# First layer's gate and value products, from the fourth pair of column blocks on, as seven block products in place of eight, on all engines in one planned order

## The chip, the cores and the metric

The kernel runs on one core of a Trainium2 chip. The metric is device microseconds of one execution; less is better. Several executions are timed, and one more is taken by the hardware profiler.

## The reference

Pooled attention (2 batches, 8 heads, 1152 tokens of 64, queries pooled in pairs) gives x of 1152 tokens x 512. A gated layer follows, the part that is changed, and then a second gated layer with eight experts:

```python
def _moe_ref(x, w_gate, w_val, w_out):      # 512 -> 1536 -> 512
    gate = 1.0 / (1.0 + np.exp(-(x @ w_gate)))
    val = x @ w_val
    return (gate * val @ w_out).astype(np.float32)
```

w_gate, w_val and w_out arrive as float64. The second layer (`_moe2_ref`) computes for each of 8 experts max(x @ w1, 0) @ w2, weighted by a routing matrix that is normalised eight times over rows and columns.

## The kernel before

All matrices are kept as two parts of a reduced float32 format, a high part (a ScalarE copy that rounds) and a low part (the rest, a subtraction). A product is three matmuls, high x high, high x low and low x high, issued by `three` (L964, matmuls on L965 to L967). x lies transposed in four tiles `x1[c]` of 128 rows (features) x 1152 columns (tokens), high and low.

There are five stretches of work. **Attention** is an order of instructions written out by a planner: each instruction is a `step` with an engine, a due time `when`, its length, what it waits for and which buffers it takes and frees; `arrange` (L219) simulates the engines and gives one order for all of them, with a table of corrections to the due times (`SHIFT`), and the program keeps it (`tc.manual_schedule`, L951). The planner also has a `port` time, within which VectorE and GpSimd operations on SBUF are not started together. The **first layer's gate and value stage** (L975 to L1018) is not planned: a loop over `fc`, 12 pairs of 128 x 2 weight columns, issues its instructions, and the compiler orders them on each engine. `gate_weights` (L985) loads and converts the weights of a pair, first one block of the gate, then one of the value. A pair is 2 (gate, value) x 4 (feature tiles c) x 3 (thirds of the tokens) x 3 = 72 matmuls of 384 columns into PSUM tiles `psb` of three banks. Then a sigmoid reads the gate's banks (L1012, ScalarE), VectorE multiplies the value's banks by it (L1013), ScalarE copies the high part of g (L1016) and GpSimd subtracts for the low part (L1017). The **output layer** (L1036 to L1067) makes four blocks of 128 output features, each 12 x 3 x 3 = 108 matmuls of 384 columns into `pso`, over g of fc 0 to 11 in that order; its weights come from the same conversion. The **second layer** is planned again (`step` on L1101): a period of 45.4 us for each of 16 halves of an expert.

`split_doubles` (L181) converts 512 float64 weight columns: a scaled copy of the upper word into PSUM (L198, ScalarE), on VectorE the sign (L199) and a shift (L200), the high part (L204, ScalarE), on VectorE what is left (L205), sign and exponent (L206) and the lower word scaled by them (L208), and GpSimd adds both into the low part (L211). Raw words have 3 buffers (`rawp`, L961), scratch tiles 2 of a kind (`conv`, L214), converted weights 2 ring slots (`ring_tile`, L969).

The second layer's first product (`first_product`, L1216) already has the form that the change brings to the first layer: x and the weights are seen as 2 x 2 blocks, and seven products of sums of blocks, A11, S1, S2, A12, S3, S4 and A22, replace eight products of blocks. A product is 2 halves of the tokens' half x 2 feature tiles x 3 = 12 matmuls of 288 columns. The products are accumulated in bank pairs X, Y and B; A11 is copied from X (or Y) to B by ScalarE (`go`), further results are copied out by ScalarE (`tap`) or added by VectorE (`add`).

## Time and profile before

| | us |
|---|---|
| median of the runs shown (1253.24, 1253.52, 1257.1) | 1253.52 |
| the profiled execution: time | 1254.48 |
| the profiled execution: span, first to last instruction | 1252.7 |
| first layer's gate and value stage in it | 287.2 to 436.9 |
| output layer, first three blocks | 436.9 to 493.0 |

Engines are PE (TensorE), PEld (its weight loads), DVE (VectorE), ACT (ScalarE), POOL (GpSimd) and SP (which issues DMAs). Busy time of PE is time with a matmul in flight; consecutive matmuls overlap, so the step from start to start, not the duration, is the cost of one. The granted clock (PEclk) is a share of 2.4 GHz. L numbers are lines of the kernel before; helper lines (L1127 for a ScalarE copy, L1130 for a two-operand operation) hold many different instructions, which are told apart by their tiles.

### The profile page before, as it was taken

To read this page: it belongs to the slowest core of one execution; us is meant where nothing else is said; L and a number is where in the kernel's file an instruction comes from. 1 tells how busy PE (TensorE), PEld (TensorE's weight loads), DVE (VectorE), ACT (ScalarE), POOL (GpSimd) and SP (SyncE) were. 2 spreads that over 40 slices of the span, in tenths; PEclk is the share of its full clock that TensorE was granted. 3 is DMA by queue.
4 is the path that set the end of the run, shared out by engine and by line. 5 is a ranking of instruction groups with operands and counts; after the bars stand their busy time and mean duration, and the time that the engine had idled before them with its cause. 6 is when DMAs were issued, how large, how long until landed. Compare 5 with 4: busy or idle time off the path is not lost.

```text
span 1252.7 us, 23722 instructions
## 1 busy us (share of the span) xinstructions
PE 1236.4 (99%) x8924; PEld 1204.6 (96%) x8924; DVE 1072.9 (86%) x1954; ACT 780.5 (62%) x1775; POOL 719.0 (57%) x751
## 2 busy tenths in 40 slices
PE   7999999999999999999999999999999999999998
PEld 7889999999999999999999999999999999999998
DVE  7999999998666674899998898898889889889887
ACT  8999999994333332657457457547556645745753
POOL 7788888674434432753574555464555556456552
PEclk9999999999999999999999999999999999999999
DMA  5112211112222232111111111111111111111112
GB/s 161 43 54 58 59 48 38 37 51 68 84 85 85 90 96 68 35 52 35 34 52 52 51 52 35 52 52 51 35 51 52 51 52 35 51 52 52 34 35 77
DMA packets 62357, 70.50 MB, mean 56 GB/s; under 512 B 3489, under 2 KB 49953, under 8 KB 62241
## 3 DMA queue, kind: packets, MB, share of 16 engines
q1 hardware_dynamic: 62240, 68.97, 18.0%
q8 instruction: 70, 1.15, 0.4%
q14 instruction: 47, 0.38, 0.1%
HBM read 66.60 MB, written 2.36 MB: 55 GB/s over the span
## 4 chain that ended last, share of the span: by engine, by line
PE 78%; DVE 14%; ACT 4%; POOL 1%; issue 1%; DMA 1%; SPq 0%; DVEq 0%; ACTq 0%; POOLq 0%
PE psb L965 4%; PE psb L967 4%; PE psb L966 4%; PE psY L965 4%; PE psY L966 4%; PE psY L967 4%; PE psX L965 4%; PE psX L966 3%; PE psX L967 3%; PE psX L1391 3%; PE psX L1396 3%; PE psX L1395 3%; DVE pT L517 3%; PE psY L1391 3%; PE psY L1396 3%; PE psY L1395 3%
## 5 line engine op out<-in xcount | busy, mean ns | idle before, releaser
L1130 POOL TENSOR_TENSOR sm<-xs 128x512 f32<-128x512 f32 x64 | 92.7, 1459 | 165.1 <-ACT xs L1127 150.2
L1127 ACT ACTIVATE w_two<-sm 128x512 fp32r<-128x512 f32 x128 | 77.8, 629 | 162.9 <-POOL sm L1130 141.2
L1130 POOL TENSOR_TENSOR sm<-raw_w 128x256 f32<-128x256 f32 x128 | 105.0, 842 | 125.1 <-DMA raw_w<-in_moe_w_dram 84.5
L536 PE MATMUL psg<-pT,vs 128*128 128x256 f32 (+1 forms) x576 | 133.4, 319 | 1.0 <-DVE pT L517 0.8
L1130 DVE TENSOR_TENSOR hb<-sm,hb 128x512 fp32r<-128x512 f32 x128 | 120.6, 969 | 9.2 <-ACT hb L1127 9.2
L1130 DVE TENSOR_TENSOR w_two<-sm,w_two 128x512 fp32r<-128x512 f32 x128 | 111.0, 874 | 5.7 <-ACT w_two L1127 5.6
L1127 ACT ACTIVATE hb<-sm 128x512 fp32r<-128x512 f32 x128 | 75.8, 626 | 55.2 <-POOL sm L1130 53.9
L1391 PE MATMUL psX<-w_two,hb 128*128 128x256 f32 x384 | 108.8, 283 | 0.2 <-DVE acc L1346 0.2
L1391 PE MATMUL psY<-w_two,hb 128*128 128x256 f32 x384 | 108.5, 283 | 0.0
L1395 PE MATMUL psX<-w_two,hb 128*128 128x256 f32 x384 | 108.3, 282 | 0.0
L1395 PE MATMUL psY<-w_two,hb 128*128 128x256 f32 x384 | 108.3, 282 | 0.0
L1396 PE MATMUL psX<-w_two,hb 128*128 128x256 f32 x384 | 108.0, 281 | 0.1
L1396 PE MATMUL psY<-w_two,hb 128*128 128x256 f32 x384 | 108.0, 281 | 0.0
L517 DVE TENSOR_TENSOR pT<-psg,pT 128x384 fp32r<-128x384 f32 x192 | 101.8, 550 | 6.7 <-ACT pT L513 4.9
L497 PE MATMUL psg<-ident,p 128*128 128x128 f32 x648 | 104.3, 273 | 1.0 <-DVE pT L517 0.8
L536 PEld LDWEIGHTS psg<-pT,vs 128*128 128x128 f32 x576 | 91.3, 189 | 4.6 <-POOL sum L549 0.9
L1130 POOL TENSOR_TENSOR sm<-raw_w,sm 128x256 f32<-128x256 f32 x96 | 95.5, 1007 | 0.3
L513 ACT ACTIVATE pT<-psg 128x384 fp32r<-128x384 f32 x192 | 90.9, 501 | 5.6 <-PE psg L497 4.3
L1130 DVE TENSOR_TENSOR w_two<-raw_w,w_two 128x512 fp32r<-128x512 f32 x96 | 73.6, 769 | 17.9 <-ACT w_two L1127 16.2
L965 PE MATMUL psb<-x,w_gv 128*128 128x384 f32 x264 | 88.2, 334 | 0.0
L966 PE MATMUL psb<-x,w_gv 128*128 128x384 f32 x264 | 88.2, 334 | 0.0
L967 PE MATMUL psb<-x,w_gv 128*128 128x384 f32 x264 | 88.2, 334 | 0.0
(282 smaller groups left out, 4731.6 us busy)
## 6 DMA issues: line engine op xcount, KB each, us to landing
raw_w<-in_moe_w_dram SPq DMA_DIRECT2D x64, 512.0 KB, 3.5
raw_o<-in_moe_w_out_dram SPq DMA_DIRECT2D x12, 512.0 KB, 3.5
raw_gv<-in_moe_w_gate_dram SPq DMA_DIRECT2D x11, 512.0 KB, 3.6
raw_gv<-in_moe_w_val_dram SPq DMA_DIRECT2D x11, 512.0 KB, 3.6
vr<-in_v_dram SPq DMA_DIRECT2D x16, 288.0 KB, 2.7
kr<-in_k_dram SPq DMA_DIRECT2D x15, 288.0 KB, 2.8
qr<-in_q_dram SPq DMA_DIRECT2D x15, 256.0 KB, 4.0
out_dram<-acc SPq DMA_DIRECT2D x18, 128.0 KB, 1.8
```

Source lines behind the costliest of these rows:

```text
L497: nc.tensor.transpose(have["tpp", i, u, g][:, n * P:(n + 1) * P], have["p", i, u][:, jj * P:(jj + 1) * P], ident)
L513: nc.scalar.activation(out=p_parts(i, u, g)[0], in_=turned(i, u, g), func=AF.Copy)
L517: nc.vector.tensor_tensor(out=lo, in0=turned(i, u, g), in1=f(hi), op=ALU.subtract)
L536: nc.tensor.matmul(have["pv", i, j, n][:, 0:HALF[n][1]], have["vs", i, j][:, jj].rearrange("p a d -> p (a d)"), have["pT", i, j, n][s][:, ...
L965: nc.tensor.matmul(ps, wh, xh, start=first, stop=False, skip_group_check=more)
L966: nc.tensor.matmul(ps, wh, xl, start=False, stop=False, skip_group_check=more)
L967: return nc.tensor.matmul(ps, wl, xh, start=False, stop=last, skip_group_check=more).ins
L1127: nc.scalar.activation(out=out_, in_=in_, func=func)
L1130: eng.tensor_tensor(out=out_, in0=a, in1=b, op=op)
L1391: nc.tensor.matmul(out_, h[:, 0, cols], w[:, 0], start=(begins and kk + m == 0), stop=False, skip_group_check=True,)
L1395: nc.tensor.matmul(out_, h[:, 0, cols], w[:, 1], start=False, stop=False, skip_group_check=True)
L1396: nc.tensor.matmul(out_, h[:, 1, cols], w[:, 0], start=False, stop=(m == 1), skip_group_check=True)
```

## The change

The first layer's gate and value stage gets a planner like the second layer's (the same `step`, now made by `planner`), with due times and a table of corrections, `SHIFT1` (571 entries, not shown). It is planned together with the conversion of the first output block's weights (`wo`). The first three units of work (NPL = 3) are computed as before, with 384 columns: gate and value 0, gate and value 1, gates 2 and 3. The nine others (values 2 and 3, gates 4 and 5, values 4 and 5, and so on) are blocks of seven products with 84 matmuls of 288 columns.

For these blocks GpSimd first adds high and low part of x again (`xq`), VectorE makes four differences of them (`tq`, each in two feature tiles), ScalarE their high parts (`th`) and GpSimd their low parts (`tl`). The conversion of a weight pair now makes whole float32 weights (`u`, GpSimd), GpSimd makes four sums of weight blocks from them, and the high and low parts of 1792 columns are made by ScalarE (`wh`) and VectorE (`wl`). VectorE adds S3 and S4 out of PSUM to earlier results (`add`). In a block of gates, sigmoids are taken by ScalarE out of PSUM or of these sums; in a block of values, VectorE multiplies A12's and A22's banks by the gate, and GpSimd multiplies the sums. The products g are kept as float32, and split later: g 0 to 3 within the plan by ScalarE and VectorE, g 4 to 11 behind it, where the high part of g takes the tile of the float32 g before it (`HOME`). Those eight splits (two low parts on GpSimd, six on VectorE) stand ahead of the output layer and are ordered by the compiler, as is all of the output layer. PSUM is eight single banks in the plan (X, Y, B and two for conversions), and the former pools are opened behind it.

```diff
+NPL = 3
...
-        def gate_weights(fc):
-            w = ring_tile(fc, f"gv{fc}")[:, :, 0:1024]
-            split_doubles(
-                w,
-                [src[:, fc * 2 * P:(fc + 1) * 2 * P].rearrange("(c p) f -> p c f", p=P) for src in (wg1, wv1)],
-                f"gv{fc}", ps_v,
-            )
-            parts[fc] = [w.rearrange("p s (i c f) -> p s i c f", i=2, c=KD)[:, :, i] for i in range(2)]
-        ring_tile(0, "gv0")
-        gate_weights(1)
-        for fc in range(NFF):
-            if fc > 1:
-                gate_weights(fc)
-            wr = parts[fc]
-            pss = []
-            for i in range(2):
-                ps = ps_b.tile([P, 3, 512], F32, tag="b", name="psb")
-                for c in range(KD):
...
+        xq = [area[f"l{8 + c}"] for c in range(KD)]
+        tx = [area[f"t{k}"] for k in range(4)]
+        gf = {fc: area[f"l{fc}"] for fc in range(8)}
+        gs = {}
...
+        HOME = ("h0", "h1"), ("h2", "l0"), ("l1", "wf"), ("l2", "sm"), *((f"l{fc - 1}", f"t{fc // 2 - 2}") for fc in range(4, NFF))
+        def home(fc, k):
+            tag = HOME[fc][k]
+            if tag[0] == "h":
+                return area[tag]
+            if tag[0] == "t":
+                if fc % 2 == 0:
+                    area["w" + tag] = g_p.tile([P, 2, N], F32R, tag=tag, name="gh")
+                return area["w" + tag][:, fc % 2]
+            return g_p.tile([P, N], F32R, tag=tag, name="gh")
+        def split_hi(fc):
+            hi = home(fc, 0)
+            gs[fc] = (hi,)
+            copy(hi, g32(fc))
+        def split_lo(fc, eng):
+            lo = home(fc, 1)
+            join(eng, lo, g32(fc), f(gs[fc][0]), ALU.subtract)
+            gs[fc] += (lo,)
+        stock1 = {
+            "raw": [rawp.tile([P, 512, 2], I32, tag="raw", name="raw_gv") for _ in range(3)],
+            "cv": [conv.tile([P, 512], F32, tag=t, name="cv") for t in ("da", "da", "ds", "ds", "dv", "dv")],
+            "w": rings,
+            "wf": [area["wf"]],
+            "sm": [area["sm"]],
+            "m": [misc.tile([P, N], F32, tag="m", name="sg") for _ in range(4)],
+        }
+            gate, val = (lambda fc: (wg1, fc)), (lambda fc: (wv1, fc))
+            units = [(gate(0), val(0)), (gate(1), val(1)), (gate(2), gate(3)), (val(2), val(3))]
+            for fc in range(4, NFF, 2):
+                units += [(gate(fc), gate(fc + 1)), (val(fc), val(fc + 1))]
+            def begins(fc):
+                return 12.5 * fc if fc < NPL else 12.5 * NPL + 10.95 * (fc - NPL)
+            def double(name, src, t, out):
...
+                    ("v", *name), "ACT", t, 530, 640,
+                    lambda: nc.scalar.activation(out=have[v], in_=f(have[raw][:, :, 1]), func=AF.Copy, scale=2.0 ** -112),
+                    [("ld", *name)], [("v", v)], [raw, v],
+                )
+                step(
+                    ("s", *name), "DVE", t + 0.7, 605, 690, lambda: nc.vector.tensor_scalar(
+                        out=have[a].bitcast(I32), in0=have[v].bitcast(I32), scalar1=SIGN, scalar2=None, op0=ALU.bitwise_and
+                    ), [("v", *name)], [("cv", a)], [v, a],
+                )
+                step(
+                    ("x", *name), "DVE", t + 1.3, 605, 690, lambda: nc.vector.scalar_tensor_tensor(
+                        out=have[a].bitcast(I32), in0=have[v].bitcast(I32), scalar=3, in1=have[a].bitcast(I32),
+                        op0=ALU.logical_shift_left, op1=ALU.bitwise_or,
+                    ), [("s", *name)], (), [v, a],
+                )
+                step(
+                    ("e", *name), "DVE", t + 1.9, 605, 690, lambda: nc.vector.tensor_scalar(
+                        out=have[v].bitcast(I32), in0=have[a].bitcast(I32), scalar1=SIGNEXP, scalar2=None, op0=ALU.bitwise_and
+                    ), [("x", *name)], (), [v, a],
+                )
+                step(
+                    ("t", *name), "DVE", t + 2.5, 605, 690, lambda: nc.vector.scalar_tensor_tensor(
+                        out=have[b], in0=have[raw][:, :, 0].bitcast(U32), scalar=2.0 ** -52, in1=have[v],
+                        op0=ALU.mult, op1=ALU.mult,
+                    ), [("e", *name)], [("cv", b)], [raw, v, b],
+                )
+                out_, gets, uses = out
+                step(
+                    ("u", *name), "POOL", t + 3.2, 1250, 1290,
+                    lambda: join(nc.gpsimd, out_(), have[a], have[b], ALU.add), [("t", *name)], gets, [a, b, *uses], port=1150,
+                )
...
+            AT = dict(A11=0, A12=256, S1=512, S2=768, S3=1024, S4=1280, A22=1536)
+            def gate_weights(fc):
+                t = begins(fc)
+                wf, sm, w = ("wf", fc), ("sm", fc), ("w", fc)
+                t0 = t - (15 if fc > NPL else 14)
+                for i, (src, col) in enumerate(units[fc]):
+                    double(
+                        (fc, i), src[:, col * 2 * P:(col + 1) * 2 * P].rearrange("(c p) f -> p c f", p=P), t0 + 2.2 * i,
+                        (lambda i=i: have[wf][:, i * 512:(i + 1) * 512], [("wf", wf)] if i == 0 else [], [wf]),
+                    )
+                u = [("u", fc, i) for i in range(2)]
+                piece = lambda tile_, a, n: (lambda: have[tile_][:, a:a + n])
+                part = lambda a, n: (lambda: have[w][:, :, a:a + n])
+                if fc < NPL:
+                    high_low((fc,), [
+                        (piece(wf, 512 * i, 512), part(512 * i, 512), 512, [u[i]], [("w", w)] if i == 0 else [], [wf, w], t - 8 + 5 * i)
+                        for i in range(2)
+                    ])
+                    return
+                b = lambda i, j: have[wf][:, (2 * i + j) * 256:(2 * i + j + 1) * 256]
+                q = lambda k: have[sm][:, k * 256:(k + 1) * 256]
+                total = (
+                    lambda: (q(0), b(1, 0), b(1, 1), ALU.add), lambda: (q(1), q(0), b(0, 0), ALU.subtract),
+                    lambda: (q(2), b(0, 0), b(1, 0), ALU.subtract), lambda: (q(3), b(0, 1), q(1), ALU.subtract),
+                )
+                for k in range(4):
+                    deps = [u[1]] if k == 0 else [("sum", fc, 0), u[0]] if k == 1 else [*u] if k == 2 else [("sum", fc, 1)]
+                    step(
+                        ("sum", fc, k), "POOL", t - 7 + (0, 0.8, 4, 4.8)[k], 700, 740,
+                        lambda k=k: join(nc.gpsimd, *total[k]()), deps, [("sm", sm)] if k == 0 else [], [wf, sm], port=580,
+                    )
+                high_low((fc,), [
+                    (piece(wf, 0, 512), part(0, 512), 512, [u[0]], [("w", w)], [wf, w], t - 6),
+                    (piece(sm, 0, 512), part(512, 512), 512, [("sum", fc, 1)], [], [sm, w], t - 4),
+                    (piece(sm, 512, 512), part(1024, 512), 512, [("sum", fc, 2), ("sum", fc, 3)], [], [sm, w], t + 1),
+                    (piece(wf, 768, 256), part(1536, 256), 256, [u[1]], [], [wf, w], t + 3),
+                ])
...
+            def operands():
+                h = lambda c, k: xq[c][:, k * HT:(k + 1) * HT]
+                for c in range(KD):
+                    step(
+                        ("xq", c), "POOL", 6 + 3 * c, 2680, 2720,
+                        lambda c=c: join(nc.gpsimd, xq[c], f(x1[c][:, 0]), f(x1[c][:, 1]), ALU.add), least=6.2 if c == 3 else 4.0,
+                        port=2500,
+                    )
+                late = 12.5 * NPL
+                for u in range(2):
+                    D1, D2 = ("xq", u), ("xq", 2 + u)
+                    todo = (
+                        (0, h(u, 0), h(u, 1), h(u, 0), [D1]),
+                        (2, h(u, 1), h(2 + u, 1), h(u, 1), [D1, D2, ("tq", 0, u)]),
+                        (1, h(2 + u, 1), h(2 + u, 1), h(u, 0), [("tq", 2, u)]),
+                        (3, h(2 + u, 0), h(2 + u, 0), h(2 + u, 1), [("tq", 1, u)]),
+                    )
+                    for n, (k, out_, a, b, deps) in enumerate(todo):
+                        t = late - 20 + 4 * n + 2 * u
+                        step(
+                            ("tq", k, u), "DVE", t, 660, 750, lambda out_=out_, a=a, b=b: join(nc.vector, out_, a, b, ALU.subtract),
+                            deps, port=630,
+                        )
+                        step(
+                            ("th", k, u), "ACT", t + 1, 585, 680, lambda k=k, u=u, out_=out_: copy(tx[k][:, 0, u], out_),
+                            [("tq", k, u)],
+                        )
+                        step(
+                            ("tl", k, u), "POOL", t + 2, 1400, 1430,
+                            lambda k=k, u=u, out_=out_: join(nc.gpsimd, tx[k][:, 1, u], out_, f(tx[k][:, 0, u]), ALU.subtract),
+                            [("th", k, u)], port=1300,
+                        )
+            def block(fc):
+                t = begins(fc)
+                a, c = ("X", "Y") if fc % 2 == 0 else ("Y", "X")
+                w, m = ("w", fc), ("m", fc)
+                (src, even), (_, odd) = units[fc]
+                gates = src is wg1
+                sg = ("sg", even), ("sg", odd)
+                part = lambda nb: slice(nb * HB, (nb + 1) * HB)
+                half = lambda tile_, k, nb: have[tile_][:, k * HT + nb * HB:k * HT + (nb + 1) * HB]
+                xin = lambda j, k: (lambda u: x1[2 * j + u][:, :, k * HT:(k + 1) * HT])
+                tin = lambda k: (lambda u: tx[k][:, :, u])
...
+                product(0, "A11", xin(0, 0), a, True, 0)
+                for nb in range(2):
+                    step(
+                        ("go", fc, nb), "ACT", t + 0.8 * (nb + 1), 295, 410,
+                        lambda nb=nb: copy(bank[f"B{nb}"][:, 0:HB], bank[f"{a}{nb}"][:, 0:HB]), ps=f"{a}{nb} B{nb}=",
+                    )
+                tl = lambda k: [("tl", k, u) for u in range(2)]
+                product(1, "S1", tin(0), c, True, 1, tl(0))
+                tap("t22", 1, c, m, 1, get=True)
+                product(2, "S2", tin(1), a, False, 1, tl(1))
+                tap("t21", 2, a, m, 0)
+                product(3, "A12", xin(1, 0), "B", False, 0)
...
+                whole("c11", 3, "B", 0, True)
+                product(4, "S3", tin(2), a, False, 2, tl(2))
+                add("c22", 4, a, 1, "t22")
+                product(5, "S4", xin(1, 1), c, False, 2)
+                add("c12", 5, c, 0, "t21")
+                product(6, "A22", tin(3), a, False, 3, tl(3))
+                whole("c21", 6, a, 1, True)
+                summed("c22", 4, 1, 1)
+                summed("c12", 5, 0, 0)
+                if not gates:
+                    done[even] = [("c11", fc, 0), ("c11", fc, 1), ("sc12", fc)]
+                    done[odd] = [("c21", fc, 0), ("c21", fc, 1), ("sc22", fc)]
+            def split_g(fc, deps, t):
+                step(("gh", fc), "ACT", t, 1050, 1140, lambda: split_hi(fc), deps)
+                step(("gl", fc), "DVE", t + 1.2, 1260, 1350, lambda: split_lo(fc, nc.vector), [("gh", fc)], port=1230)
+            done = {}
+            operands()
+            for fc in range(NFF):
+                if fc:
+                    gate_weights(fc)
+                (plain if fc < NPL else block)(fc)
+            end = begins(NFF)
+            last = [("wl", NFF - 1, k) for k in range(4)]
+            split_g(0, done[0], end - 45)
+            split_g(1, [*done[1], ("gl", 0)], end - 34)
+            split_g(2, [*done[2], *last, ("gl", 1)], end - 7)
+            split_g(3, [*done[3], *last, ("gl", 2)], end - 4)
...
+            with tc.manual_schedule(engines=engines):
+                for s in arrange(steps, stock1, 30e3):
+                    for what, kind, slot in s["got"]:
+                        have[what] = stock1[kind][slot]
+                    s["emit"]()
+        ps_b = pbs.enter_context(tc.tile_pool(name="ps_b", bufs=2, space=PSUM, reuse_waits="tile"))
+        ps_v = pbs.enter_context(tc.tile_pool(name="ps_v", bufs=2, space=PSUM, reuse_waits="tile"))
+        for fc in range(4, NFF):
+            split_hi(fc)
+            split_lo(fc, nc.gpsimd if fc in (7, 10) else nc.vector)
 
...
-            w = ring_tile(c, f"o{c}")[:, :, 0:NFF * P]
-            split_doubles(
-                w,
-                [
-                    wo1[g * GRP * P:(g + 1) * GRP * P, c * 2 * P:(c + 1) * 2 * P].rearrange("(a p) e -> p a e", p=P)
-                    for g in range(NFF // GRP)
-                ],
-                f"o{c}", ps_v,
-            )
+            if c:
+                w = ring_tile(c + 1, f"o{c}")[:, :, 0:NFF * P]
+                split_doubles(w, [wo_part(c, g) for g in range(NFF // GRP)], f"o{c}", ps_v)
+            else:
+                w = have["wo"][:, :, 0:NFF * P]
```

## Rows read from the trace of the kernel before

**Rows 1.** The page, part 1: busy time of each engine, share of the span, instructions.
```profile
PE 1236.4 (99%) x8924; PEld 1204.6 (96%) x8924; DVE 1072.9 (86%) x1954; ACT 780.5 (62%) x1775; POOL 719.0 (57%) x751
```
**Rows 2.** Windows: length; busy time and instructions of PE, PEld, DVE, ACT, POOL; clock; DMA share, GB/s.
```profile
287.20:436.90 149.70, 149.70 (x866) 149.70 (x865) 97.94 (x145) 58.35 (x77) 64.42 (x41) 1.00 0.27 85
436.90:493.00 56.10, 56.10 (x326) 56.10 (x325) 34.30 (x51) 15.26 (x24) 17.08 (x12) 1.00 0.30 94
```
**Rows 3.** Timeline of PE: start us, duration us; 384-column matmuls, then 288-column ones.
```profile
287.23 0.42 PE L965 MATMUL psb<-x,ks 128*128 128x384 f32 x1
...
437.10 0.33 PE L965 MATMUL pso<-gt,w_o 128*128 128x384 f32 x1
...
568.58 0.29 PE L965 MATMUL psB<-xb,w_two 128*128 128x288 f32 x1
...
570.17 0.29 PE L965 MATMUL psY<-xc,w_two 128*128 128x288 f32 x1
```
**Rows 4.** Timeline at the end of attention: the last attention operation of POOL.
```profile
292.08 0.88 POOL L594 TENSOR_TENSOR x<-sw,x 64x320 fp32r<-64x320 f32 x1
```
**Rows 5.** Instructions by line and form, 287 to 440 us: busy us, mean ns; idle before, releasers.
```profile
L1017 POOL TENSOR_TENSOR gt<-sg,gt 128x1152 fp32r<-128x1152 f32 x11 | 29.6, 2688 | 57.1 <-ACT gt L1016 57.1
L211 POOL TENSOR_TENSOR w_gv<-da_gv,ds_gv 128x512 fp32r<-128x512 f32 x22 | 28.4, 1291 | 22.5 <-DVE ds_gv L208 22.5
L1013 DVE TENSOR_TENSOR sg<-psb,sg 128x1152 f32<-128x1152 f32 x12 | 16.3, 1357 | 19.3 <-PE psb L967 15.8 <-issue 3.4
...
L198 ACT ACTIVATE dv_gv<-raw_gv 128x512 f32<-128x512 f32 x22 | 14.0, 636 | 17.9 <-DVE ds_gv L208 13.0 <-DMA raw_gv<-in_moe_w_val_dram 3.9 <-DVE sw L583 0.6
...
L1016 ACT ACTIVATE gt<-sg 128x1152 fp32r<-128x1152 f32 x11 | 12.9, 1169 | 6.0 <-DVE sg L1013 6.0
```
**Rows 6.** The same view, 530 to 1240 us (second layer), for DVE, ACT and POOL.
```profile
L1130 DVE TENSOR_TENSOR hb<-sm,hb 128x512 fp32r<-128x512 f32 x127 | 118.9, 962 | 9.2 <-ACT hb L1127 9.2
L1130 DVE TENSOR_TENSOR w_two<-sm,w_two 128x512 fp32r<-128x512 f32 x123 | 107.0, 878 | 2.3 <-ACT w_two L1127 2.2
...
L1130 DVE TENSOR_TENSOR xs<-psY,xs 128x288 f32<-128x288 f32 x62 | 26.7, 448 | 2.3 <-PE psY L967 2.3
...
L1127 ACT ACTIVATE xs<-psY 128x288 f32<-128x288 f32 x94 | 37.3, 407 | 16.4 <-PE psY L967 16.4
...
L1130 POOL TENSOR_TENSOR sm<-raw_w 128x256 f32<-128x256 f32 x121 | 98.4, 834 | 125.1 <-DMA raw_w<-in_moe_w_dram 84.5 <-issue 17.6 <-DVE w_two L1130 12.0
```
**Rows 7.** Timeline of DVE in the changed stage and the output layer.
```profile
304.11 0.69 DVE L205 TENSOR_TENSOR da_gv<-dv_gv,w_gv 128x512 f32<-128x512 f32 x1
304.72 0.69 DVE L206 TENSOR_SCALAR dv_gv<-dv_gv 128x512 int32<-128x512 int32 x1
305.32 0.69 DVE L200 SCALAR_TENSOR_TENSOR dv_gv<-dv_gv,ds_gv 128x512 int32<-128x512 int32 x1
...
311.03 0.69 DVE L199 TENSOR_SCALAR ds_gv<-dv_gv 128x512 int32<-128x512 int32 x1 [1.07 <-ACT dv_gv L198]
...
312.50 1.36 DVE L1013 TENSOR_TENSOR sg<-psb,sg 128x1152 f32<-128x1152 f32 x1
...
458.28 0.75 DVE L178 TENSOR_TENSOR xa<-xs,xa 128x576 fp32r<-128x576 f32 x1
```
**Rows 8.** Windows of two periods of the second layer, columns as in rows 2.
```profile
575.40:620.80 45.40, 43.79 (x329) 41.88 (x328) 44.09 (x94) 25.39 (x57) 25.77 (x24) 1.00 0.16 47
...
1029.40:1074.80 45.40, 45.40 (x351) 44.85 (x350) 40.10 (x68) 27.30 (x62) 24.41 (x24) 1.00 0.15 47
```
**Rows 9.** Timeline in the second layer: a POOL operation and a DVE operation started within it.
```profile
598.28 1.29 POOL L1130 TENSOR_TENSOR sm<-xs 128x512 f32<-128x512 f32 x1 [1.88 <-DVE rs L1572]
598.31 1.29 DVE L1573 TENSOR_SCALAR rs<-rs 128x9 f32<-128x9 f32 x1
```
**Rows 10.** Weight loads of two tiles: count, duration ns min/median/max, first and last start.
```profile
L965 PEld LDWEIGHTS psb<-x,w_gv x264: 187/188/188, 299.7 to 436.4; 128*128 128x128 f32 x132
...
L965 PEld LDWEIGHTS psX<-xa,w_two x12: 187/188/191, 627.1 to 671.9; 128*128 128x128 f32 x12
```

262 lines of the change are left out of this document (218 added, 44 removed), and 90 rows, old and new, of the table SHIFT1.

## The prediction

> **What bounds the kernel now.** I read three things in this order: the page's busy times, then the windows of each stage, then single instructions of the stage that is changed. The page says that TensorE has a matmul in flight for 99% of the span [rows 1]. A busy TensorE need not be at its peak, so the windows come next. In the first layer's stage (287.2 to 436.9 us) and in the output layer behind it TensorE is busy for the whole of the stretch at the full granted clock, while VectorE has 97.94 of 149.70 us, ScalarE 58.35 and GpSimd 64.42 [rows 2]. So here the matmul stream alone sets the end, and only fewer matmul columns can shorten it.
>
> The price of a column comes from start to start, since durations overlap. The stage's first matmul starts at 287.23, the output layer's first at 437.10 [rows 3]: 149.87 us for 12 pairs of 72 matmuls, so 12.49 us a pair and 173.5 ns for 384 columns. The MoE layers already run 288-column matmuls of the kind that the change brings: one product of 12 goes from 568.58 to 570.17 [rows 3], 132.5 ns each. The ratio 0.764 is close to 288/384 = 0.75, so a narrower matmul is charged nearly by its columns.
>
> **What the change is worth if TensorE stays full.** Three pairs stay as they are. Nine become blocks of 7 products x 12 matmuls: 84 x 132.5 ns = 11.13 us in place of 12.49. 9 x 1.36 = **12.2 us** go. The profiled execution took 1254.48 us, 0.96 over the median of 1253.52; by the median the floor is 1253.5 - 12.2 = 1241.3. Everything below is what may be given back.
>
> **Start of the stage and operand sums: 0 to 2 us, I take 0.5.** GpSimd ends attention at about 293.0 [rows 4], 5.8 us into the stage. Before the third product of the first block (37.5 + 3.2 = 40.7 us in) it must do four 1152-wide sums of x at the price of L1017 (4 x 2.69), six 512-wide joins for the three weight pairs at L211's 1.29, six 576-wide low parts (1.45 each, scaled from 1.29) and two 256-wide weight sums (at most 0.83) [rows 5, 6]: 5.8 + 10.8 + 7.7 + 8.7 + 1.7 = 34.7 us. It fits with 6 us to spare; VectorE's eight subtractions (0.75, L178) and ScalarE's eight copies lie beside the plain pairs [rows 7]. If the spare is eaten by waits, the block starts late by the rest; I bound that with 2.
>
> **VectorE in the blocks: 0 to 6 us, I take 2.5.** 512-wide operations start 0.60 us apart [rows 7]. From the first block to the end of the stage (100.2 us) VectorE has: conversions of eight pairs, 8 x 2 x 4 x 0.60 = 38.4; low parts of the 1792 weight columns, 8 x (3 x 0.60 + 0.35) = 17.2; 56 reads of 288 columns out of PSUM (36 sums, 20 gate-times-value), at 0.448 busy [rows 6] some 0.42 apart, 23.5; four 1152-wide low parts of g, near L1013's 1.36 [rows 5], 5.0; the first output weights, 15 x 0.60 = 9.0. That is 93.1 us, of which 6 (the later two thirds of those weights) may run past the end. In the MoE stage operations with two SBUF inputs take 0.96 and 0.88 us against 0.69 undisturbed [rows 6, 7], a wait of 0.2 to 0.3; at 0.25 the 36 such operations add 9. Needed in time, then: 93.1 - 6 + 9 = 96 of 100.2. The MoE stage shows both sides of this: a window with VectorE at 40.10 of 45.40 loses nothing on TensorE, one at 44.09 loses 1.61 [rows 8]. The latter scaled to 100 us is 3.5, and 2.5 lies between the two, nearer to the fuller. Where it would show: the next block's first product writes the bank whose last sum VectorE reads during A22, a cover of 1.59 us for two reads of 0.45; a low part that waits ahead of them eats it. The upper end takes such a loss of 0.65 in each of nine blocks.
>
> ScalarE has at most some 9 us in a block of 11.1 (two conversions, four weight copies, six to ten 288-wide reads at 0.41 [rows 5, 6], two 576-wide sigmoids) and hides behind the products; without that cover only a 0.41 read a product would show. The same 25 loads go out on SP, each into a raw buffer freed by the same kind of VectorE operation as now and several us ahead of use; nothing is issued on GpSimd's queue. Loads of the second output weights queue behind the planned ones, as they do now. I cost these at nothing.
>
> **End of the stage: 0.3 to 9 us, I take 2.** Eight of the twelve g are split only behind the plan, and in a chain: the high part of g 4 is written over the float32 tile of g 3, whose low part must have read it, and so on. A link is a 1152-wide copy, 1.17 us (L1016), a subtraction of 1.27 (L1013 less the overlap) and hops of some 0.1: 2.5; the two links on GpSimd take 1.17 + 2.69 + 0.1 = 3.95 [rows 5]. 6 x 2.5 + 2 x 3.95 = 22.9 us. VectorE is free for it when its planned work ends, 0 to 4 us behind the last matmul; at 1.5 the last g is there at 24.4, whereas TensorE would ask for it after 11 x 1.56 = 17.2 us. Walked in strict order, TensorE loses 7.2 (5.7 and 9.7 at the ends). But this part is not planned by hand, and today's order there isn't the order of the source: conversions of the fourth pair run at 311.03, ahead of the second pair's gate product at 312.50, though the loop issues them two turns later [rows 7]. If TensorE's order is made likewise, 36 matmuls (6.2 us) of the second output block fill the gap as soon as its first weights are there. Then 0.3 to 3 are lost. I take 2; the new PSUM pool, which must wait for the last bank reads, is inside it.
>
> Sum: 12.2 - 0.5 - 2.5 - 2 = 7.2 us gained; 1253.5 - 7.2 = **1246.3**.
>
> **Rivals.**
> *The chain of splits is not covered (0.20).* For it: no row shows TensorE's own order changed. Against: VectorE's and ScalarE's are. 12.2 - 0.5 - 2.5 - 7.2 = 2.0 gained: 1251.5, no measurable change.
> *All is hidden (0.15).* Most MoE windows lose nothing at 88% of VectorE [rows 8]. 1241.3 to 1243.
> *The SBUF lock between VectorE and GpSimd makes VectorE the bound (0.09): slower.* A 9-element operation takes 1.29 us, just as long as the GpSimd operation that started 0.03 before it [rows 9]. Two blocks last 22.3 us and hold 16 x 0.60 + 2 x 2.15 + 12 x 0.42 = 18.9 us of VectorE work, so the slack is 3.4 for eight low parts: 0.42 a wait. Beyond it each wait falls on TensorE, 36 times. With the 2.5 of the stage's two ends (0.5 and 2), the gain is gone at 0.42 + 9.7/36 = 0.69. At 0.90 the result is 36 x 0.48 - 9.7 = 7.6 slower, 1261; at a full 1.29, 1275. Against: the mean wait now is 0.2 to 0.3 [rows 6]. The Trainium skill, SBUF — State Buffer, "SBUF: two separate sides", calls the shared port pair an exclusive lock held for a whole instruction; the 1.29 us agree with that, and by this rule the full 1.29 is what every low part could meet.
> *The weight loads bound the stream (0.02): slower.* They are busy for all of the stage (188 ns each at a pitch of 173.5) [rows 2, 3, 10]. The change raises their number from 648 to 756; if each cost a pitch of 173.5 ns, 18.7 us would be added: 1272. Against, decisively: the same 188 ns loads stand in the 288-column stream [rows 10] at a pitch of 132.5, so they overlap. The Trainium skill, Perfetto Trace Analysis, "Identifying the Most-Contended Engine", wants TensorE's headroom judged by the share of weight-load time; the profile page's 96% [rows 1] would say there is none here, and the pitch disagrees.
>
> **How the numbers follow.** The likeliest case, 0.54, gives 1246.3 (own range 1243 to 1250). About 0.3% (3.8 us) is what a measurement can tell from no change, so faster means below 1249.7: most of the likeliest (0.50), all of the hidden case (0.15), a little of the uncovered chain (0.05): 0.70. Slower: the two slow rivals, 0.11. Same: 0.19. The range goes from the floor, 1241.3, to 1253.5, which takes in the uncovered chain with up to 5 us lost in the stage ahead of it; about 0.15 is left out.
>
> **What would show it.** Right: from the stage's first matmul to the output layer's first some 140.7 us (137.7 + 3); 288-column products 1.59 us apart; VectorE above 90% busy between them; in the output layer a hole in TensorE before the matmuls of g 7 to 11, or matmuls of the second block between them. Wrong: a stage of 150 us or more with VectorE named as releaser (the lock), holes ahead of S1 or S2 in the first block (late sums of x), 5 us or more lost behind the stage (the chain), or a pitch of 288 columns above 140 ns.

## The result, and the profile after

The changed kernel takes 1267.79 us (median of four runs, 1265.78 to 1268.08) against 1253.51 for the kernel before: ratio 1.0104 [1.0083, 1.0125], 1.0% slower. The prediction, 1246.3 in 1241.3 to 1253.5, was wrong in sign. The profiled execution took 1267.68 us, its span is 1265.9, 13.2 more than the 1252.7 of before.

L numbers in rows from here on are lines of the kernel that ran. In after, L1058 to L1060 are the three matmuls of a product, L1097 is ScalarE's copy or sigmoid and L1100 a two-operand operation on VectorE or GpSimd. The page's busy times, as [rows 1] of before:

```profile
PE 1234.5 (98%) x9032; PEld 1197.0 (95%) x9032; DVE 1122.3 (89%) x2040; ACT 811.9 (64%) x1879; POOL 760.5 (60%) x799
```

TensorE's share fell by a point only, so the page doesn't say where 13 us went. Windows do. Of after, in the manner of [rows 2]: the stage's first 59.5 us, its rest, and the output layer (length, then busy time and instructions of each engine, granted clock, DMA share, GB/s):

```profile
287.50:347.00 59.50, 53.88 (x324) 51.44 (x323) 56.95 (x82) 28.34 (x55) 51.59 (x36) 1.00 0.26 81
347.00:435.60 88.60, 87.78 (x654) 86.61 (x653) 83.11 (x143) 55.59 (x122) 55.00 (x52) 1.00 0.28 89
435.60:517.80 82.20, 78.65 (x432) 77.49 (x433) 44.64 (x61) 24.30 (x33) 30.69 (x25) 0.96 0.20 65
```

In the first window VectorE is busy for 56.95 of 59.50 us and GpSimd for 51.59, and TensorE alone has gaps. In the second VectorE is nearly as full and TensorE loses almost nothing. In the third VectorE, ScalarE and GpSimd are idle for about half of the time or more, and the clock is not at its full level: here something waits in a chain.

The holes, from TensorE's timeline (start, duration, instruction, and in brackets the idle time before it and who ended it), nine of them in order of time; the last two are the second layer's first two that waited:

```profile
301.15 0.44 PE L1058 MATMUL pmX<-x,w_gv 128*128 128x384 f32 x1 [0.88 <-ACT w_gv L1097]
315.41 0.44 PE L1060 MATMUL pmX<-x,w_gv 128*128 128x384 f32 x1 [0.39 <-DVE w_gv L1100]
330.47 0.40 PE L1058 MATMUL pmY<-x,w_gv 128*128 128x288 f32 x1 [1.17 <-ACT sg L1097]
338.50 0.40 PE L1060 MATMUL pmY<-tx,w_gv 128*128 128x288 f32 x1 [1.50 <-DVE w_gv L1100]
435.59 0.44 PE L1058 MATMUL pso<-gh,w_gv 128*128 128x384 f32 x1 [0.46 <-DVE gt L1100]
454.94 0.45 PE L1059 MATMUL pso<-gh,w_gv 128*128 128x384 f32 x1 [2.71 <-POOL gh L1100]
457.53 0.69 PE L1059 MATMUL pso<-gh,w_gv 128*128 128x384 f32 x1 [0.53 <-DVE gh L1100]
523.33 0.61 PE L1058 MATMUL psX<-xa,w_two 128*128 128x288 f32 x1 [4.88 <-ACT w_two L1097]
525.00 0.61 PE L1060 MATMUL psX<-xa,w_two 128*128 128x288 f32 x1 [0.82 <-DVE w_two L1100]
```

They make three places. Each is counted from start to start of matmuls, beyond 173.5 and 132.5 ns.

| place | before | after | difference |
|---|---|---|---|
| stage: first product to output layer's first | 149.87 | 148.06 | -1.8 |
| output layer: its first to the second layer's first matmul (`psB`) | 74.88 | 82.23 | +7.35 |
| from there to the second layer's first product (`psX`) | 0.47 | 5.51 | +5.0 |
| losses in the second layer's next 22 us | 0.5 | 3.1 | +2.6 |

The stage should have gained 12.2 and gained 1.8: 8.2 of the missing 10.4 lie ahead of 347, and 2.3 behind it. With 0.3 for a later start the table gives 13.4, against the 13.2 measured.

Behind the long holes TensorE runs at its lower clock for a while (the granted clock is the third number from the right):

```profile
456.00:462.00 6.00, 5.47 (x19) 4.95 (x18) 3.96 (x5) 2.24 (x4) 1.28 (x1) 0.54 0.26 87
522.00:527.00 5.00, 2.85 (x10) 2.51 (x11) 4.94 (x7) 4.71 (x11) 1.41 (x1) 0.50 0.15 22
```

0.50 is 1.2 GHz, so a hole can be paid a second time: of the output layer's 7.35 about 4.2 us are the holes and the rest is the clock. It isn't paid each time. In a run below (e5) the same wait of 2.71 us was followed by the full clock, and that output layer took 79.64 us in place of 82.23:

```profile
454.35 0.45 PE L1059 MATMUL pso<-gh,w_gv 128*128 128x384 f32 x1 [2.71 <-POOL gh L1100]
454.35:460.35 6.00, 5.24 (x28) 4.92 (x29) 3.99 (x6) 3.49 (x5) 1.29 (x1) 1.00 0.26 83
```

### The profile page after: what moved, and what is told of

Same layout as the page of the kernel before. It is cut to its first block, busy times and chain, and to the rows that moved or that the text cites. A ratio compares the mean times of both kernels' runs of the same rounds, so it can differ in the third digit from the quotient of the medians.

```text
span 1265.9 us, 24188 instructions
## 1 busy us (share of the span) xinstructions
PE 1234.5 (98%) x9032; PEld 1197.0 (95%) x9032; DVE 1122.3 (89%) x2040; ACT 811.9 (64%) x1879; POOL 760.5 (60%) x799
## 4 chain that ended last, share of the span: by engine, by line
PE 60%; DVE 6%; ACT 1%; issue 1%; POOL 0%; DVEq 0%; ACTq 0%
PE psY L1058 4%; PE psY L1059 4%; PE psY L1060 4%; PE psX L1058 4%; PE psX L1060 4%; PE psX L1059 4%; PE psX L1871 4%; PE psX L1876 3%; PE psX L1875 3%; PE psY L1871 3%; PE psY L1876 3%; PE psY L1875 3%; PE psB L1058 1%; PE psB L1059 1%; PE psB L1060 1%; PE psB L1871 1%
## 5 line engine op out<-in xcount | busy, mean ns | idle before, releaser
L1100 POOL TENSOR_TENSOR sm<-xs 128x512 f32<-128x512 f32 x64 | 92.6, 1458 | 167.2 <-ACT xs L1097 152.9
L1100 POOL TENSOR_TENSOR sm<-raw_w 128x256 f32<-128x256 f32 x128 | 103.8, 833 | 125.6 <-DMA raw_w<-in_moe_w_dram 84.1
L1097 ACT ACTIVATE w_two<-sm 128x512 fp32r<-128x512 f32 x128 | 77.7, 629 | 156.8 <-POOL sm L1100 135.2
L1100 DVE TENSOR_TENSOR hb<-sm,hb 128x512 fp32r<-128x512 f32 x128 | 119.4, 960 | 9.0 <-ACT hb L1097 9.0
L1100 DVE TENSOR_TENSOR w_two<-sm,w_two 128x512 fp32r<-128x512 f32 x128 | 112.1, 883 | 1.4 <-ACT w_two L1097 1.2
L1097 ACT ACTIVATE hb<-sm 128x512 fp32r<-128x512 f32 x128 | 75.8, 626 | 54.8 <-POOL sm L1100 53.5
L1100 POOL TENSOR_TENSOR sm<-raw_w,sm 128x256 f32<-128x256 f32 x96 | 91.8, 970 | 0.3
L1100 DVE TENSOR_TENSOR hb<-xs,hb 128x512 fp32r<-128x512 f32 x96 | 88.8, 937 | 0.0
L1100 DVE TENSOR_TENSOR w_two<-raw_w,w_two 128x512 fp32r<-128x512 f32 x96 | 73.9, 772 | 15.9 <-ACT w_two L1097 14.1
L590 PEld LDWEIGHTS psg<-ident,p 128*128 128x128 f32 x648 | 78.5, 140 | 6.8 <-issue 0.9
L582 POOL TENSOR_SCALAR p<-p,sum 128x672 f32<-128x672 f32 x72 | 60.3, 837 | 35.1 <-ACT sum L578 32.9
```

What stands on the lines that cost most here:

```text
L590: nc.tensor.transpose(have["tpp", i, u, g][:, n * P:(n + 1) * P], have["p", i, u][:, jj * P:(jj + 1) * P], ident)
L1097: nc.scalar.activation(out=out_, in_=in_, func=func)
L1100: eng.tensor_tensor(out=out_, in0=a, in1=b, op=op)
```

## The experiments

Profiled executions differ by up to 3.2 us in where the stage begins (286.2 to 289.4 us), so lengths of stretches are compared and totals only beside them. "Stage" is from its first matmul to the output layer's first. e1 to e10 were timed once each, e11 to e13 five times.

### The second layer's start: ring slots

The plan hands out the two weight slots as they fall free: fc 1 takes slot 0, fc 11 again slot 0, the output layer's first block (`wo`) slot 1, and its last block then slot 0. Before, the last block had slot 1. The second layer's first weight tiles lie on slot 0's memory.

```diff
-            "w": rings,
+            "w": rings[::-1],
...
-                w = ring_tile(c + 1, f"o{c}")[:, :, 0:NFF * P]
+                w = ring_tile(c, f"o{c}")[:, :, 0:NFF * P]
```

> Edit: the two ring slots are handed out in the other order, so that the third and fourth output blocks lie in the same slots as before the change and the second layer's first weight tiles, which overlay the ring, come free as early as its planner takes them to. Theory (slot order): the hole of 4.9 us and the cold stretch behind it at the start of the second layer go; the time from the output layer's last matmul to the second layer's steady stream falls by 7 to 8 us; total 1259.5 to 1261. Rival (the second layer's weights come late because SPq and VectorE are late behind the longer output layer, or because the g tiles under its buffers were moved): nothing changes there; total 1266 to 1268. Stage and output layer unchanged in both.

1258.33 us (e1), 9.4 less than after's profiled run; from `psB` to `psX` 0.47 us again. The two losses of the second layer's start are gone, 7.8 us. Most of the rest is the output layer's (79.98 us): the same hole of 2.71 us is in it, but the granted clock over the 6 us behind it was 0.74, in after 0.62, so 2.3 us of the gain come with the clock there and don't belong to the second layer's start. ScalarE's first copy of a second-layer weight, of after and of this kernel:

```profile
518.07 0.72 ACT L1097 ACTIVATE w_one<-raw_w 128x256 fp32r<-128x256 f32 x2 [13.40 <-PE psy L1060]
```

```profile
502.98 0.71 ACT L1097 ACTIVATE w_one<-raw_w 128x256 fp32r<-128x256 f32 x2
```

In after ScalarE stands for 13.40 us until the output layer's last matmul has read the slot; with the slots exchanged it waits for nothing. The cause of this loss is shown. It has nothing to do with seven products: it is who gets which buffer at the end of a stage.

### The output layer: the chain of splits

```diff
-        HOME = ("h0", "h1"), ("h2", "l0"), ("l1", "wf"), ("l2", "sm"), *((f"l{fc - 1}", f"t{fc // 2 - 2}") for fc in range(4, NFF))
+        HOME = ("h0", "h1"), ("h2", "l0"), ("l1", "wf"), ("l2", "sm"), *((f"l{3 if fc == 4 else fc - 2}" if fc != 5 else "m", f"t{fc // 2 - 2}") for fc in range(4, NFF))
...
+            if tag == "m":
+                return misc.tile([P, N], F32R, tag="m", name="gh")
```

The high part of g now takes the tile of the g two before it, and g 5 a free scratch tile, so there are two chains in place of one.

> Edit: one of the eight late splits writes its high part into a free scratch tile, so that each high part waits for the low part two g before it, not for the one just before. Theory (serial chain of splits): the holes in the first output block (0.6, 3.0, 0.9 us, and 2.9 us at half clock behind them) go, the output layer takes 75 to 76 us in place of 82.2; total 1260 to 1262. Rival (VectorE is overloaded at the end of the stage by conversions and the splits come late whatever they wait for): the holes stay within 2 us of what they were; total 1266 to 1268.

1264.25 us (e2). The output layer takes 76.03 us; behind its first matmul it no longer waits. What it loses is 1.1 us, where after lost 7.3, and that is the clock (0.53 from 437.9 to 440.3, behind the hole shown next). So the chain is the cause of the holes. But the stage grew to 150.46 us, by this:

```profile
427.15 3.73 DVE L1100 TENSOR_TENSOR gh<-gt,gh 128x1152 fp32r<-128x1152 f32 x2
434.76 0.44 DVE L1100 TENSOR_TENSOR sg<-pmY,sg 128x288 f32<-128x288 f32 x1
```

```profile
435.26 0.40 PE L1058 MATMUL pmY<-tx,w_gv 128*128 128x288 f32 x1 [1.77 <-DVE sg L1100]
```

Splits that are free to go early were put by the compiler ahead of VectorE's last planned reads of PSUM, and the last product waits for one of those.

Both edits together:

> Edit: both earlier ones together, the ring slots in the other order and the free tiles that break the chain of splits behind the plan. If the losses of the second layer's start and of the output layer are separate, both holes are gone: 9.4 us from the first and 3.4 from the second less than the changed kernel's 1267.7, some 1255, with the loss of the stage (about 10 us, two of them at its end) all that remains. If one hides the other, the time is that of the ring order alone, 1258.

1256.89 us (e7), with attention 1.9 us longer in this execution (granted clock 0.97 in its first 50 us). Output layer 75.02, 0.47 to `psX`, stage 150.51. The two losses are separate and add up; what is left is the stage.

### The stage: what makes the holes of the first 60 us?

Four edits tried one suspect each: sums of x in halves (e3); a planner that knows when the engines come free (e5); the bank that the blocks begin on (e6); the earliest start of the sums (e8). The four expectations below stand in this order.

```diff
# e3_xhalf
-                        lambda c=c: join(nc.gpsimd, xq[c], f(x1[c][:, 0]), f(x1[c][:, 1]), ALU.add), least=6.2 if c == 3 else 4.0,
...
+                            lambda c=c, cols=cols: join(
+                                nc.gpsimd, xq[c][:, cols], f(x1[c][:, 0, cols]), f(x1[c][:, 1, cols]), ALU.add
+                            ), least=6.2 if c == 3 else 4.0, port=1300,
...
# e5_start
-                for s in arrange(steps, stock1, 30e3):
+                for s in arrange(steps, stock1, 30e3, busy=dict(DVE=3400, POOL=5800, ACT=1500)):
...
# e6_bank
-                a, c = ("X", "Y") if fc % 2 == 0 else ("Y", "X")
+                a, c = ("X", "Y") if fc % 2 == 1 else ("Y", "X")
...
# e8_xqlate
-                        lambda c=c: join(nc.gpsimd, xq[c], f(x1[c][:, 0]), f(x1[c][:, 1]), ALU.add), least=6.2 if c == 3 else 4.0,
+                        lambda c=c: join(nc.gpsimd, xq[c], f(x1[c][:, 0]), f(x1[c][:, 1]), ALU.add), least=(11.0, 13.7, 16.4, 19.1)[c],
...
```

> Edit: the four sums of x on GpSimd, 1152 wide (2.7 us each), are made as eight of 576 (1.43 each). Theory A (in the first 60 us VectorE waits for the SBUF lock behind long GpSimd operations, up to 2.4 us a time): the holes of the stage's first 60 us fall from 8.8 to 4 to 6 us, and no VectorE operation of 512 lasts over 2.2 us there; total 1263 to 1265. Theory B (the plan takes VectorE and GpSimd to be idle at its start, but attention holds them for 3.4 and 5.8 us more): little change, 8 to 9 us. Theory C (GpSimd simply has too much to do): no change or a little worse, since eight operations take 11.4 in place of 10.8 us.

> Edit: the planner is told that VectorE is free 3.4 us, GpSimd 5.8 us and ScalarE 1.5 us after the start of the stage, as the trace shows; nothing else. Theory B (the plan's order is wrong for the real start): the holes of the first 60 us fall from 8.8 to under 5 us; total 1262 to 1264. Theory A or C (lock, or GpSimd's volume): the holes only move, 8 to 10 us are lost as before; total 1266 to 1269.

> Edit: the blocks of seven products begin on bank pair X where they began on Y and the other way round, so that the first block does not begin on the banks that the last plain pair of columns has just filled. Theory C (the two holes of 0.56 and 1.33 us ahead of the first block wait for the sigmoids that read those banks): both go, 1.5 to 2 us less in all. Theory A (VectorE and GpSimd are late there anyway): the holes move to another wait and the time stays within 0.7 us.

> Edit: the four sums of x on GpSimd may not start before 11 us into the stage (they could start at 4), so that the low parts of the second pair's weights come ahead of them. Theory A, in its narrow form (the first two sums, 5.3 us, delay the second pair's weights): the holes of 1.04 and 0.67 us at the second pair go, and the first block is not later; 1.7 us less. Rival: GpSimd has no room left behind, so the same time is lost ahead of the first block, and the total stays within 0.7 us.

None helped. Stage lengths: 151.09, 148.56, 150.30 and 153.25 us against 148.06; totals 1269.11, 1264.38, 1266.33 and 1269.87 (e5's 3.3 less lie outside the stage: it began 1.1 earlier, and the output layer took 79.64, without the lower clock behind its hole). All but e5 moved the holes; the first 60 us still lost 8.1 to 10.1 us. One hole of each of e3, e6 and e8:

```profile
308.08 0.69 PE L1058 MATMUL pmY<-x,w_gv 128*128 128x384 f32 x1 [3.82 <-ACT sg L1097]
```

```profile
331.20 0.40 PE L1058 MATMUL pmY<-tx,w_gv 128*128 128x288 f32 x1 [1.70 <-ACT sg L1097]
```

```profile
303.23 0.69 PE L1060 MATMUL pmX<-x,w_gv 128*128 128x384 f32 x1 [2.44 <-DVE w_gv L1100]
```

In e6 the first of the two waits for sigmoids went and the second grew from 1.17 to 1.70: the sigmoid itself is late, whichever bank it reads. The named releaser is the last of a queue of late work.

The next edit takes work away: the sums of x on GpSimd are left out, and the differences are made from x's high parts.

```diff
-                        lambda c=c: join(nc.gpsimd, xq[c], f(x1[c][:, 0]), f(x1[c][:, 1]), ALU.add), least=6.2 if c == 3 else 4.0,
...
+                hi = lambda c, k: f(x1[c][:, 0, k * HT:(k + 1) * HT])
...
-                        (0, h(u, 0), h(u, 1), h(u, 0), [D1]),
+                        (0, h(u, 0), hi(u, 1), hi(u, 0), []),
```

> Edit: the four 1152-wide sums of x on GpSimd are left out, and the differences are made from x's high parts alone (so x's low part is missing from S1 to S4 and A22); 10.8 us less work for GpSimd in the first 37 us of the stage. Theory A (GpSimd's fullness and the waits of VectorE behind its 1152-wide operations make the holes of the first 60 us): those holes fall from 8.8 us to 2 to 4 us, the fc=1 weights' hole (1.7) and the weights' holes of the third and fourth block go, the time falls by 5 to 7 us. Theory B (the holes come from the planned order itself: PSUM banks and due times): the holes fall by less than 2 us.

Stage 145.47, 2.6 less; losses of the first 60 us 5.2 in place of 8.2 (the 8.8 of the expectations is these 8.2 and the 0.6 at the stage's end); total 1261.98 (e4). The total fell by 5.7 as theory A had it, but only 2.6 of that is the stage: 2.3 are the output layer, with less of the lower clock, and 0.8 an earlier start. Between the two theories, then: 10.8 us of GpSimd's work were worth 3.0 us of losses. Work matters, but these sums are not the whole of it.

The last three kernels here leave the amount of work for the first block alone, and two of them change the time that there is for it. The first block comes behind four plain pairs in place of three, so 12.5 us later, for 1.36 us of the gain. Due times and earliest starts of the sums are worked out anew, with the engines busy at the start. Ring slots as above; the splits of g 4 to 11 are steps of the plan, on the two chains.

```diff
-NPL = 3
+NPL = 4
...
+            for fc in range(4, NFF):
+                split_g(
+                    fc, [*done[fc], *([("gl", 3 if fc == 4 else fc - 2)] if fc != 5 else [*done[10], *done[11]])], end - 9 + SPG * (fc - 4),
...
```

> Edit: ring slots in the other order, the splits of g 4 to 11 inside the plan on free tiles, four plain pairs in place of three (so 12.5 us more between attention and the first block, for 1.36 us of the gain), and a new table of due times, worked out with GpSimd and VectorE busy at the start and with the lock between them in the order in which they ask. Theory A (the holes of the first 60 us are there because VectorE's and GpSimd's work for the first block is crammed into 37.5 us in which both are full): nearly all holes go, from the stage's first matmul to the output layer's first 140 to 142 us, the time 1244 to 1247, faster than both kernels. Rival (VectorE, slowed by the lock with GpSimd, is the bound of the whole stage): the holes come back in the blocks, the stage stays at 145 us or more and the time at 1250 or more.

1248.15 us (e9), 1.2 above the expectation; stage 141.80, the losses of the first 60 us 0.07 us, output layer 75.01. In this kernel the sigmoids of one half of g 7 and g 11 run behind the products that use them; the next two kernels wait for them (and rename PSUM banks), one with three plain pairs and one with four:

> Edit: as the kernel with four plain pairs (ring slots exchanged, splits of g inside the plan, due times worked out anew with both engines busy at the start), but with three plain pairs, as in the change; PSUM banks renamed so that the output layer's first tile doesn't take the banks that are read last. Theory A (the work for the first block doesn't fit into three plain pairs, whatever the order): 3 to 6 us of holes remain in the first 60 us, stage 141 to 144 us, time 1248 to 1252. Rival (it was only the order, the table of due times): under 1 us of holes, stage 138 to 139 us, 1245 to 1247, better than with four plain pairs.

> Edit: four plain pairs, ring slots exchanged, splits of g inside the plan, PSUM banks renamed, and every sum taken through a sigmoid before it is used in the next block. By theory A the stage takes its columns alone, 4 x 12.49 + 8 x 11.13 = 139.0 us, and up to 2 more; the output layer 75 us and the second layer's start without a hole as in the kernel before: 10 us gained of the 10.9 that eight blocks can give, some 1243 to 1247. Rival (VectorE slowed by the lock is the bound of the blocks): 1250 or more.

Three pairs (e10): 1254.29 us, stage 147.47, 8.0 us lost ahead of 347, so more than either of its expectations had. Four pairs (e11): 1248.62 us (1247.44 to 1248.71), ratio to before 0.9947 [0.9933, 0.9960]; the stage is as expected, the total 1.6 above. The same window of both, and the four-pair kernel's whole stage:

```profile
287.50:347.00 59.50, 54.29 (x321) 52.43 (x321) 57.54 (x84) 26.98 (x52) 48.79 (x36) 0.97 0.25 80
```

```profile
287.50:347.00 59.50, 59.50 (x361) 59.50 (x362) 56.23 (x89) 30.59 (x59) 53.74 (x36) 1.00 0.32 99
287.76:427.00 139.24, 139.24 (x964) 139.24 (x962) 127.82 (x214) 80.02 (x164) 106.47 (x81) 1.00 0.29 91
```

This is the reading that matters: with four pairs VectorE (56.23) and GpSimd (53.74) are as busy in this window as in after (56.95 and 51.59), and TensorE loses nothing. The whole stage is 139.24 us, and 4 x 12.49 + 8 x 11.13 = 139.0. So a busy share does not tell whether holes come. Nor is equal busy time equal work, for it holds the time that an operation stands behind the other engine. Measured against the quickest tenth of operations of its shape, VectorE's operations that start in this window took 11.5 us too long in after and 11.1 in e10, but 3.9 in e11. These waits alone don't set the holes either: with halved sums (e3) they were 8.5 us and the losses no smaller, and e9 has 5.9 without a loss.

What goes with the losses in every run is how many plain pairs stand ahead of the first block. In their first 60 us the kernels with three lost 8.0 to 10.1 us (5.2 without the sums of x); the four kernels with four pairs, each with a table of its own, lost 0.1, 0.1, 3.1 and 2.0 (e9, e11, e12, e13). So the holes come with work that is due before it can be done, and 12.5 us more ahead of it take them away. How much of it is the amount of work and how much the waits that come with the crowding was not separated. That three pairs can't hold the work in any order isn't shown either: two tables were tried there, the change's (e1 to e8 are variants of it) and e10's.

### What is left behind the stage

The four-pair kernel e11 still takes 79.21 us in the output layer, of which 2.5 are one hole and most of the rest above 75 the lower clock behind it. TensorE's row, GpSimd's for the weights it waits for, and what GpSimd and VectorE do ahead of them:

```profile
448.73 0.48 PE L1049 MATMUL pso<-gh,w_o 128*128 128x384 f32 x1 [2.50 <-POOL w_o L293]
```

```profile
447.40 1.27 POOL L293 TENSOR_TENSOR w_o<-da_o,ds_o 128x512 fp32r<-128x512 f32 x1 [7.70 <-DVE ds_o L290]
437.03 2.67 POOL L1089 TENSOR_TENSOR gh<-gt,gh 128x1152 fp32r<-128x1152 f32 x1
437.06 3.86 DVE L1089 TENSOR_TENSOR gh<-gt,gh 128x1152 fp32r<-128x1152 f32 x1 [2.00 <-ACT gh L1086]
```

The second block's weights come behind the splits, and a split on VectorE (1.35 alone) that starts 0.03 behind one on GpSimd takes 3.86.

> Edit: the kernel with four plain pairs, but all splits of g on VectorE (none on GpSimd), the float32 tile of g 5 split into a free scratch tile as soon as that is free, and due times worked out anew, so that VectorE and ScalarE are through with the plan's work 13.6 us behind the last block in place of about 16. If the hole of 2.5 us (and the half clock behind it, 5.0 in all) ahead of the second output block is VectorE and GpSimd being late with that block's first weights, because splits stand ahead of them: the hole is under 1 us, the output layer takes 75 to 76.5 us in place of 80, and the time is 1243.5 to 1245.5. Rival (that block's weights are late by their own chain of conversions): the hole stays above 1.5 us and the time at 1247 or more.

1258.73 us (e12; 1256.9 to 1260.1), ratio 1.0035 [1.0021, 1.0049]. The text above is not what ran: the two splits of g 7 and g 10 had stayed on GpSimd. The hole ahead of the second block is gone all the same, but a new one opened at the output layer's start. It makes 6.9 of the stage's 150.70 us (3.1 more were lost in its first 60), and the lower clock behind it makes the output layer 77.57:

```profile
436.94 0.69 PE L1049 MATMUL pso<-gh,w_gv 128*128 128x384 f32 x1 [6.86 <-DVE gt L1091]
```

```profile
435.03 1.49 DVE L1091 TENSOR_TENSOR gh<-gt,gh 128x1152 fp32r<-128x1152 f32 x1
436.44 0.45 DVE L1091 TENSOR_TENSOR gt<-pmB,sg 128x288 f32<-128x288 f32 x1
```

A read of 0.45 us that frees the output layer's PSUM tile stands behind splits and weights on VectorE, since nothing in the plan waits for it. With that wait counted, and now with all eight late splits on VectorE:

> Edit: the kernel with four plain pairs (label e11_four), but now really with all eight late splits on VectorE, none on GpSimd, and due times worked out anew with the last bank reads counted as what the output layer's first matmul waits for. Theory (the losses behind the stage are VectorE's order, not the amount of its work): nothing is lost at the output layer's start (under 0.5 us) nor ahead of its second block (under 1 us); stage 139 to 140 us, output layer 75 to 76 us, time 1243 to 1245.5. Rival (splits and weights together are more than VectorE can do there): 3 us or more lost ahead of the second block again, 1247 or more.

1247.77 us (e13; 1246.82 to 1249.17), ratio to before 0.9942 [0.9928, 0.9955]; the output layer:

```profile
430.39:505.30 74.91, 74.91 (x434) 74.91 (x434) 56.14 (x75) 31.73 (x47) 29.43 (x25) 1.00 0.22 71
```

No loss there, with two splits more on VectorE than in e11: it was not the amount of its work. That e12 lost the hole ahead of the second block with both splits still on GpSimd says that the order alone can do it. The stage took 142.61 (3.6 lost, 2.0 of them ahead of 347), so the total missed its expectation by 2.3 us: the new order of the end came with another order of the beginning. e11's stage (139.24) with this output layer would make some 1244.4; it wasn't run.

## Why the prediction was wrong

**The full gain, 12.2 us: right.** Where nothing waits, the stage is its columns (139.24 against 139.0 in e11, for eight blocks; nine never ran without a wait).

**"Start of the stage and operand sums: 0 to 2 us, I take 0.5": this step failed most.** 8.2 us were lost ahead of 347. It asked whether GpSimd has the sums of x ready in time, and no hole waits for those: S1 of the first block loses nothing. What came late is what had to share the two engines with them: weights of the second and third pair (301.15, 315.41), a sigmoid of the last plain pair (330.47), S3's weights (338.50). For these it had no term. It added up GpSimd's work alone and found 6 us to spare; VectorE's work of that stretch was never added up, though it is busy there for 56.95 of 59.50 us, and by the count above some 11.5 of these went in 12 operations, beside each of which one of GpSimd ran: waits that the step put at nothing. The two meet in the lock that the third rival names. Three of VectorE's operations that met one on GpSimd, with the latter (576 wide: 0.75 alone [rows 7]; 512 wide: 0.68):

```profile
296.00 2.67 POOL L1100 TENSOR_TENSOR gt<-x 128x1152 f32<-128x1152 f32 x1
296.11 3.17 DVE L1100 TENSOR_TENSOR gt<-gt 128x576 f32<-128x576 f32 x1
304.71 2.68 POOL L1100 TENSOR_TENSOR gt<-x 128x1152 f32<-128x1152 f32 x1
304.73 3.20 DVE L1100 TENSOR_TENSOR w_gv<-gt,w_gv 128x512 fp32r<-128x512 f32 x1
318.00 1.29 POOL L1100 TENSOR_TENSOR gt<-cv 128x512 f32<-128x512 f32 x1
318.13 1.71 DVE L1100 TENSOR_TENSOR w_gv<-gt,w_gv 128x512 fp32r<-128x512 f32 x1
```

Waits of 2.4, 2.5 and 1.0 us, not the 0.2 to 0.3 of [rows 6]; the first two stood behind sums of x. The bound of 2 came from one engine's spare time; the right question was whether everything due before 40 us could be done with both engines taking turns. Taking the sums away gave back 3.0 of 8.2 us (e4), 12.5 us more time and a new order gave back all (e11).

**VectorE in the blocks, 2.5 taken: near, but only from 347 on.** 2.3 us were lost there, 0.6 of them at the stage's end, with VectorE busy for 83.11 of 88.60. Of the 8.2 ahead of 347, 3.1 lie ahead of the first block and 5.0 within it and the start of the second; counted with the blocks, these would put this term past its upper end of 6.

**End of the stage: the size right, the cover wrong.** The chain in strict order was worked out as 7.2 us; it cost 7.35. Taken was 2, by "if TensorE's order is made likewise": the compiler had moved VectorE's and ScalarE's work, and I let it move TensorE's. It didn't, in any run. This rival had 0.20 and was the one that happened, beside two losses that it didn't include. That the size agrees was luck: 7.35 holds about 3 of lower clock, which the sum didn't have, and the holes alone are 4.2. With the same wait of 2.71 and the full clock behind it e5 lost 4.8. The place was right: the holes stand ahead of g 9, 10 and 11.

**The second layer's start: missed altogether.** "I cost these at nothing" was said of loads and of the output layer's other weights; that the new plan hands out the ring slots in another parity, and that the second layer's tiles lie on slot 0, was not looked at. 7.6 us (5.0 and 2.6), all undone by e1.

**Its own signs.** Of the signs that it named for being wrong one came as it was told, more than 5 us lost behind the stage. The first block had holes too, but not the ones it named: they stand at A11 and within S3, S1 loses nothing, S2 0.3 us to a copy on ScalarE, and none of them waits for sums of x. The pitch of 132.5 ns and the stage's columns held.

**The rivals.** Slower it was, but not by the mechanism of the slower rivals as they stand. The lock is there, costs up to 2.5 us a time and took 11.5 us of VectorE's time at the start of the stage, where no rival looked; it didn't make VectorE the bound of the blocks, as e11 shows with no more than 0.2 us lost in its whole stage. The weight loads bound nothing: 139.24 of 139.24 us busy in e11, and the stage takes just its columns.

In sum 12.2 - 8.16 - 2.26 - 7.35 - 7.6 = -13.2, by which the measured span grew.

## What to carry to other kernels

A cheaper inner product is only worth what its preparation leaves: add up for every engine, not the likeliest one, what is due before the first use, and count the turns that VectorE and GpSimd take, which a busy share hides; starting the new form one unit later can be worth more than that unit. Follow buffers over the end of the changed stage, who holds which slot and what is laid over it next, since a change of parity there cost 7.6 of the 12.2 us that the change could give. And let no order be hoped for: where the program gives no order, assume the one of the source for TensorE.

## What the runs showed of the hardware

VectorE's wait behind GpSimd is about as long as what GpSimd has left in hand: operations of 0.75 and 1.35 us took 3.17 and 3.86 when GpSimd had just begun one of 2.67. The Trainium skill, SBUF — State Buffer, "SBUF: two separate sides", calls the shared port pair an exclusive lock for a whole instruction, and these rows agree. The prediction had the lock as a small rival and priced it with the mean wait of another stage.

Behind idle stretches of 2.71 and 4.88 us of TensorE the granted clock of after was 0.54 from 456 to 462 us and 0.50 from 522 to 527 us, 0.50 being its 1.2 GHz level, and some 3 and some 1.5 us more were lost behind them. The length of the idle stretch doesn't tell it: behind 2.71 us in e5 the clock stayed at 1.00, behind 1.77 us in e2 it was 0.53.
